# Gated linear attention and a low-rank mixer: the first batch's attention written in another order, halves of units one step behind, the mixer's start in pieces

## The chip, the cores and the metric

The kernel runs on one core of one Trainium2 chip, in fp32. The metric is device time in microseconds (us), the median of several executions. "PE" is TensorE's matrix unit, "DVE" VectorE, "ACT" ScalarE, "POOL" GpSimd, and "SP" SyncE, which here only issues DMA transfers.

## What is computed

There are 4 batches, 8 heads, 768 positions, a head width of 48, a model width of 384 and a mixer rank of 32. The attention keeps a 48x48 state for each head, which a gate of its own for each row lets decay, and reads it with q:

```python
f = 1.0 / (1.0 + np.exp(-f_logit))
for t in range(S):
    state = f[:, :, t, :, None] * state + np.einsum('bhd,bhe->bhde', k[:, :, t], v[:, :, t])
    y[:, :, t] = np.einsum('bhd,bhde->bhe', q[:, :, t], state)
```

The heads side by side are x (4, 768, 384), and the mixer follows:

```python
xt = x.transpose(0, 2, 1)
h = xt @ U @ V                                # U 768x32, V 32x768
u = x + h.transpose(0, 2, 1)
ch = np.maximum(u @ w_ch1, 0.0) @ w_ch2       # 384x1536 and 1536x384
return u + ch
```

## The kernel before

**Units and their pieces.** The work of the attention is cut into 16 units. Unit n is one pair of heads of one batch, four units (`HP`) for each batch. A unit has a front, `prepare(n)`, and a rear, `attend(n)`, and each returns a list of functions, its pieces.

The front has five pieces:

- `gates`: the gate logits f are turned so that time runs along the free axis, and ACT makes the sigmoid `fz` of them. In the first two batches PE does the turning with six transposes (`on_tensor`, L466), and ACT reads PSUM (L487, L488). From batch 2 on (`TURNED`) DVE turns them within SBUF (`turned`, L448), and ACT reads that (L493, L494).
- `keep`: a scan on DVE that runs backwards through each chunk of 64 steps, `X` (L498), with three small DVE operations (L505 to L508) and a small ACT copy (L503).
- `keys`: k turned and multiplied by X, `kz` (L478; from batch 2 on L448 and L481).
- `read_back`: the forward scan `Y` on DVE (L515).
- `queries`: q turned and multiplied by Y, `qT` (L478, or L448 and L481). At its end it issues the transfers of f, k, q and v of unit n+2 on SP (L520, `load` L349), since f, k and q have two buffers.

The rear has five pieces:

- `kept`: PE turns kz back (L568), and ACT copies it to `kb` (L572).
- `states`: ACT spreads the chunks' decays to `whole` (L576), PE forms the chunks' contributions `ds` from kb and v (L584), ACT copies them to `added` (L590), and a DVE scan makes all states `st` (L597).
- `scores`: PE multiplies k and q within each chunk, `sc` (L547), and DVE masks it to `A` (L554).
- `read`: PE reads the states with q, `y` (L612), and ACT makes a small copy, `seen` (L619).
- `inner`: PE adds A times v to the same y (L630), and ACT copies y to `x` (L636).

**The mixer.** The class `Mixer` gives the pieces of a batch. `low_rank` is `ph` on PE (L136) and its copy `h` on ACT (L139). `mix(t)`, for six blocks t of 128 positions, is `pu` on PE (L148), which DVE adds to x (`add`, L144). `turn(t)` is `put`, three transposes on PE (L157), copied to `uT` by ACT (L159). `ch1(a, j)`, for three pairs a of blocks and six j, is `pz` on PE, six matmuls for one (a, j) (L167; the profile has two records of each fp32 matmul), whose positive part ACT writes to `z` (L174). The second product of the first batch is `ch2`, `po` (L189), of which DVE makes the output `o` (L144); later batches use `seven`, `pw` (L212), on sums that DVE forms.

**Weights.** U, V, w1 and w2 come as 8-byte floats. `start` (L51) issues the transfer, and `end` (L56) converts: two ACT operations (L63, L64), three on DVE (L65, L66, L67) and one on POOL (L68), with two buffers `w_y`. `ahead_by` issues the transfer of the ninth weight tile on at each conversion. The first six pieces of w1 land in a buffer of the mixer (`place`, L427), others in four `w_raw`.

**PSUM.** `ps_big` has three buffers for the attention, `ps_mm` two for the mixer.

**What sets the order.** PE's order is the program's order throughout. That of DVE and ACT is the program's in batches 0 and 1 up to the start of the second batch's mixer (the `manual_schedule` at L678); after that a scheduler orders them, and it may also place later work on DVE and ACT among earlier work. SP and POOL are ordered by the scheduler everywhere. `add`, A and st carry a higher priority.

The first batch begins with unit 0's front and unit 1's gates (L681). Then each n takes, in this order (L689):

```python
pieces = [kept, keep, keys, read_back, states, scores, gates, read, queries, inner]
```

where kept, states, scores, read and inner are of unit n, keep, keys, read_back and queries of unit n+1, and gates of unit n+2. For the last n the conversions of U and V stand in the places of the front. Then comes the first batch's mixer, L702: low rank, six `mix`, six `turn`, then `ch1` for all a at each j. Every third of the first thirteen pieces, and each later one, has a weight conversion ahead of it (L703).

In `attention(b, todo)` (L644) the same interleaving, with unit n's rear and unit n+1's front, runs for later batches. Between the pieces `Fill` puts pieces of the previous batch's mixer, in proportion to their cost. `start_mixer` (L662) places the last of those among the `ph`, `pu` and `put` of the batch just attended.

Of the kernel before, what the change touches and what calls it, by code (L numbers as in the profile page):

```python
# [9 lines left out]
F32 = mybir.dt.float32  # L10
# [286 lines left out]
def factored_path(ctx, tc, q, k, v, f_logit, moe_U, moe_V, moe_w_ch1, moe_w_ch2, out, ok):  # L297
# [23 lines left out]
    TURNED = 2  # L321

    assert S % (2 * P) == 0 and H % 2 == 0 and NB < D <= PAD and PAD == 2 * NB and S % NB == 0 and W == NBL * 2 * PAD
    assert DM % P == 0 and FF % P == 0 and FF % WP == 0 and DM == WP and DM <= 512 and R % 32 == 0 and P % R == 0 and P // R <= NBL and NFC % 4 == 0
    assert NBL * PAD <= 512 and C == PAD

    const = ctx.enter_context(tc.tile_pool(name="const", bufs=1))
# [48 lines left out]
                    )  # L376

    load(0, "f", "k", "q")
    load(1, "f", "k")
    load(0, "v")  # L380
    load(1, "q", "v")

    ident = const.tile([P, P], F32, name="ident")
    make_identity(nc, ident)
# [61 lines left out]
    def turned(t, src_tile):  # L446

        nc.vector.transpose(  # L448
            t.rearrange("p (c i) -> p c i", i=NB), src_tile.rearrange("p (c d) -> p c d", d=NB),
        )  # L450
# [3 lines left out]
    def prepare(n):  # L454
# [4 lines left out]
        r, f = raw[n % 2], fz[n % 2]  # L459
        by_chunk = f[:, 0:S].rearrange("p (c t) -> p c t", t=C)  # L460

        def on_tensor(nm):

            pt = ps_big.tile([P, 2, 512], F32, name="pt", tag="big")
            for c in range(NBL):
                nc.tensor.transpose(  # L466
                    pt[:, 2 * c // NBL, c % (NBL // 2) * P : (c % (NBL // 2) + 1) * P],
                    nat[n % 2][nm][:, c].rearrange("p h d -> p (h d)"), ident,
                )
            return pt[:, :, 0 : G * C].rearrange("p a (c t) -> p a c t", t=C)  # L470
# [12 lines left out]
        def gates():  # L483
            f0 = T["f0"] = two.tile([P, NCH], F32, name="f0")
            if b < TURNED:
                pt = on_tensor("f")
                nc.scalar.activation(halves(f)[:, :, :, 1:C], pt[:, :, :, 1:C], AF.Sigmoid)  # L487
                nc.scalar.activation(f0.rearrange("p (a c) -> p a c", a=2), pt[:, :, :, 0], AF.Sigmoid)  # L488
                return
            fT = one.tile([P, S], F32, name="fT")  # L490
            turned(fT, r["f"])
            fv = fT.rearrange("p (c t) -> p c t", t=C)
            nc.scalar.activation(by_chunk[:, :, 1:C], fv[:, :, 1:C], AF.Sigmoid)  # L493
            nc.scalar.activation(f0, fv[:, :, 0], AF.Sigmoid)  # L494
# [14 lines left out]

        def keys():  # L510
            operand("k", "X")

        def read():
            Y = T["Y"] = one.tile([P, S], F32, name="Y")
# [1 line left out]

        def queries():
            operand("q", "Y")
            if n + 2 < NU:
                load(n + 2, "f", "k", "q", "v")  # L520

        return [gates, keep, keys, read, queries]

# [5 lines left out]
    def attend(n):  # L529
# [42 lines left out]
            nc.scalar.copy(kb.rearrange("p h c d -> p h (c d)"), pt[:, :, 0 : NBL * PAD])  # L572

        def states():
            whole = one.tile([P, D, NCH], F32, name="whole")
            nc.scalar.copy(whole, wholes[n % 2].unsqueeze(1).broadcast_to((P, D, NCH)))  # L576

            ds = ps_big.tile([P, 2, 512], F32, name="ds", tag="big")
            for c in range(NBL):
                for s in range(2):  # L580
                    for par in range(2):

                        i = (c + (s & par)) % NBL
                        nc.tensor.matmul(  # L584
                            ds[par * PAD : (par + 1) * PAD, s, c * D : (c + 1) * D],
                            lhsT=T["kb"][part[s ^ par], par, i, :], rhs=vt[part[s ^ par], c, par, :],
                            start=True, stop=True,
                        )

            nc.scalar.copy(  # L590
                added[:, 1:].rearrange("p (e c s) -> p e c s", c=NBL, s=2),
                ds[:, :, 0 : NBL * D].rearrange("p s (c e) -> p e c s", e=D),
            )

            st = two.tile([P, D * NCH], F32, name="st")
            with tc.high_priority(offset=AHEAD):
                nc.vector.tensor_tensor_scan(  # L597
                    st, added[:, 0 : D * NCH], whole.rearrange("p e c -> p (e c)"), 0.0, ALU.add, ALU.mult
                )
            T["st"] = st.rearrange("p (e c) -> p c e", c=NCH)  # L600

# [37 lines left out]
            )  # L639
            del units[n], v_tiles[n]  # L640

        return [kept, states, scores, read, inner]

    def attention(b, todo):  # L644


        fill = Fill(todo, HP * 10)
        for n in range(b * HP, (b + 1) * HP):
            kept, states, scores, read, inner = attend(n)
            if n + 1 < NU:  # L650
                gates, keep, keys, read_back, queries = prepare(n + 1)
                order = [gates, kept, keep, keys, states, scores, read_back, read, queries, inner]
                if (n + 1) // HP >= TURNED:
                    order[0:2] = [kept, gates]
            else:
                order = [kept, states, scores, read, inner]
            for piece in order:
                fill()
                piece()
        fill.rest()  # L660

    def start_mixer(b, after):  # L662
# [14 lines left out]
    ctx.enter_context(tc.manual_schedule(engines={nc.tensor.engine}))  # L677
    with tc.manual_schedule(engines={nc.vector.engine, nc.scalar.engine}):  # L678

        ready = {n: prepare(n) for n in range(2)}  # L680
        for piece in ready[0] + ready[1][:1]:  # L681
            piece()
        for n in range(HP):
            kept, states, scores, read, inner = attend(n)
            _, keep, keys, read_back, queries = ready.pop(n + 1, [lambda: None] * 5)
            if n + 2 < HP:
                ready[n + 2] = prepare(n + 2)
            gates = ready[n + 2][0] if n + 2 < HP else lambda: None
            pieces = [kept, keep, keys, read_back, states, scores, gates, read, queries, inner]  # L689
            if n == HP - 1:  # L690

                pieces[1:4] = loads[: early - 1]
                pieces[-2] = loads[early - 1]
            for piece in pieces:
                piece()
            if n == 0:

                loads = ahead_by(early + FIRST, weights)
        loads = loads[early:]

        m = mixer(0)
        for i, (_, piece) in enumerate(m.before + m.firsts):  # L702
            if loads and (i % 3 == 0 or i >= len(m.before)):  # L703
                loads.pop(0)()
            piece()
        for f in loads:
            f()
        n = len(m.seconds) // (NBL // 2)
        todo, after = m.seconds[:-n], m.seconds[-n:]
        for piece in prepare(HP):  # L710
            piece()
            todo.pop(0)[1]()
        attention(1, todo)
        m = start_mixer(1, after)
        for f in to_sum:
            f()
# [336 lines left out]
```

## Time and profile before

| | us |
|---|---|
| median of 3 runs | 539.18 |
| lowest and highest | 538.66, 539.69 |
| the profiled execution | 539.65 |
| its span | 537.9 |
| PE busy | 504.1 (94%) |
| DVE busy | 268.6 (50%) |
| ACT busy | 144.8 (27%) |
| POOL busy | 33.5 (6%) |
| start of `ph` of the first batch | 56.30 |
| its first `pu`, first `pz`, end of its last `pz` | 59.73, 71.26, 117.96 |
| PE idle before the first `ph`, of 56.3 | 18.1 |
| end of the second batch's last `put` | 208.1 |

The profile is of one execution, and its span leaves out 1.75 us of that execution's time. The page cuts the span into 40 slices of 13.4 us; a digit is the busy share in tenths, and PEclk is the granted clock of TensorE in tenths of full speed. A line of the waits names who waited, for whom, and then the total, how often, and the longest, in us. A line of a timeline has the start, the duration, the engine, the line of the kernel and the operation; in brackets the engine's idle time before it and what ended it. Both engines that matter here show a duration that overlaps with the next by some 0.1 us, so that a series of operations advances by a little less than the sum of its durations.

### The profile page before, as it was taken

What the parts mean: (1) busy time and instruction counts of PE and PEld (TensorE: products, weight loads), DVE (VectorE), ACT (ScalarE), POOL (GpSimd) and SP (SyncE); (2) the same over time, 40 slices, a digit from 0 to 9 for tenths busy, and PEclk for the clock granted to TensorE, in tenths of its full rate; (3) what the DMA queues carried; (4) which work ended last, traced back from release to release, by engine and by line L of the source; (5) the groups of instructions that cost most, each with busy time, mean ns of one, the idle gap of its engine ahead of it and who ended that gap; (6) DMA issues with size and microseconds to landing.
All of it is one profiled execution on the core that took longest, in us unless ns stands there. A gap on an engine that the chain in (4) does not pass through costs nothing.

```text
span 537.9 us, 11981 instructions
## 1 busy us (share of the span) xinstructions
PE 504.1 (94%) x5277; PEld 416.5 (77%) x5277; DVE 268.6 (50%) x406; ACT 144.8 (27%) x293; POOL 33.5 (6%) x49
## 2 busy tenths in 40 slices
PE   5677889999997999999999999999999999999995
PEld 4566378886775547889899777898899868998995
DVE  5675575556667856467575740745403340222232
ACT  3233375561322203232331204220311112202010
POOL 3001243331000000000000000000000000000000
PEclk9875599999999799999999999999999999999999
DMA  9977945524556335032713603010000000000000
GB/s 146 162 155 188 189 114 162 160 78 86 106 88 86 56 63 82 1 56 38 116 22 65 86 0 67 1 24 30 2 2 32 1 30 1 1 29 1 11 20 35
DMA packets 149334, 34.88 MB, mean 65 GB/s; under 512 B 139801, under 2 KB 147481, under 8 KB 149273
## 3 DMA queue, kind: packets, MB, share of 16 engines
q1 hardware_dynamic: 149272, 34.03, 33.6%
q8 instruction: 43, 0.70, 0.6%
q14 instruction: 19, 0.15, 0.1%
HBM read 29.29 MB, written 4.72 MB: 63 GB/s over the span
## 4 chain that ended last, share of the span: by engine, by line
PE 83%; DVE 7%; SPq 4%; ACT 2%; DMA 1%; issue 1%; DVEq 0%; ACTq 0%
PE pz L167 35%; PE pw L212 22%; PE po L189 8%; PE y L612 4%; PE pt L466 3%; PE pu L148 2%; PE y L630 2%; SPq L367 2%; SPq L373 2%; PE ds L584 2%; PE sc L547 1%; PE pt L568 1%; PE put L157 1%; PE ph L136 1%; ACT uT L159 1%
## 5 line engine op out<-in xcount | busy, mean ns | idle before, releaser
L167 PE MATMUL pz<-uT,w 128*128 128x256 f32 x864 | 192.8, 382 | 0.8 <-ACT uT L159 0.7
L167 PEld LDWEIGHTS pz<-uT,w 128*128 128x128 f32 x864 | 162.3, 190 | 23.9 <-ACT uT L159 1.0
L174 ACT ACTIVATE z<-pz 128x512 f32<-128x512 f32 x63 | 37.6, 597 | 130.4 <-PE pz L167 126.3
L212 PE MATMUL pw<-zw,w_raw 128*128 128x192 f32 x324 | 56.2, 328 | 0.8 <-DVE o L144 0.8
L212 PE MATMUL pw<-w,z 128*128 128x192 f32 x324 | 56.2, 328 | 0.0
L212 PEld LDWEIGHTS pw<-zw,w_raw 128*128 128x128 f32 x324 | 52.8, 190 | 2.4 <-DVE o L144 2.1
L212 PEld LDWEIGHTS pw<-w,z 128*128 128x128 f32 x324 | 52.9, 190 | 1.5 <-DVE x L144 0.7
L144 DVE TENSOR_TENSOR w_raw<-z 128x768 f32<-128x768 f32 x18 | 17.2, 953 | 58.7 <-ACT z L174 58.6
L498 DVE TENSOR_TENSOR_SCAN X<-fz,ends 128x768 f32<-128x768 f32 x16 | 28.0, 1750 | 17.7 <-ACT fz L487 13.2
L597 DVE TENSOR_TENSOR_SCAN st<-added,whole 128x576 f32<-128x576 f32 x16 | 21.6, 1351 | 26.4 <-ACT added L590 26.4
L612 PE MATMUL y<-st,qT 48*64 48x48 f32 x704 | 21.2, 275 | 8.4 <-DVE st L597 8.4
L612 PEld LDWEIGHTS y<-st,qT 48*64 48x64 f32 x704 | 18.4, 170 | 12.8 <-issue 11.2
L515 DVE TENSOR_TENSOR_SCAN Y<-fz,starts 128x768 f32<-128x768 f32 x16 | 28.0, 1753 | 0.2
L68 POOL TENSOR_TENSOR w<-w_y,w_r 128x384 int32<-128x384 int32 x24 | 25.3, 1055 | 40.9 <-DVE w_y L67 39.5
L189 PE MATMUL po<-w,zw 128*128 128x384 f32 x72 | 27.2, 524 | 0.0
L189 PE MATMUL po<-w,z 128*128 128x384 f32 x72 | 25.3, 495 | 0.2 <-DVE x L144 0.2
L65 DVE TENSOR_SCALAR w_y<-w_y 128x384 f32<-128x384 f32 (+1 forms) x27 | 11.1, 409 | 27.0 <-ACT w_y L63 27.0
L148 PE MATMUL pu<-h,V 128*128 128x384 f32 x48 | 21.4, 570 | 1.7 <-ACT h L139 0.7
L189 PEld LDWEIGHTS po<-w,zw 128*128 128x128 f32 x72 | 13.8, 201 | 9.0 <-issue 1.8
L144 DVE TENSOR_TENSOR w_y<-w_y,pw 128x192 f32<-128x192 f32 x18 | 6.3, 350 | 28.7 <-PE pw L212 28.7
L144 DVE TENSOR_TENSOR w_y<-x,pw 128x192 f32<-128x192 f32 x9 | 3.2, 350 | 34.3 <-ACT w_y L225 34.3
L148 PEld LDWEIGHTS pu<-h,V 128*128 128x128 f32 x48 | 9.0, 210 | 13.8 <-DVE x L144 7.6
(92 smaller groups left out, 526.2 us busy)
## 6 DMA issues: line engine op xcount, KB each, us to landing
w_raw<-in_moe_w_ch_dram SPq DMA_DIRECT2D x18, 384.0 KB, 3.1
out_dram<-o SPq DMA_DIRECT2D x24, 192.0 KB, 2.1
f_raw<-in_f_logit_dram SPq DMA_DIRECT2D x16, 144.0 KB, 4.0
k_raw<-in_k_dram SPq DMA_DIRECT2D x16, 144.0 KB, 4.2
q_raw<-in_q_dram SPq DMA_DIRECT2D x16, 144.0 KB, 3.9
v_nat<-in_v_dram SPq DMA_DIRECT2D x16, 144.0 KB, 3.3
v_nat<-in_v_dram SPq DMA_DIRECT2D x32, 72.0 KB, 3.1
zw<-in_moe_w_ch_dram SPq DMA_DIRECT2D x6, 384.0 KB, 13.0
```

The lines of the kernel that those rows point to most:

```text
L68: nc.gpsimd.tensor_tensor(dst.bitcast(I32), shaped(y.bitcast(I32)), shaped(r), ALU.add)
L144: nc.vector.tensor_tensor(*args)
L148: nc.tensor.matmul(pm[:, 0:DM], lhsT=V[:, t * P : (t + 1) * P], rhs=h[0], start=True, stop=True)
L167: nc.tensor.matmul(pm[:, i * 2 * P : (i + 1) * 2 * P], lhsT=w1[:, m, o : o + P], rhs=uT[a][:, m, :], start=(m == 0), stop=(m == NDC - 1))
L174: nc.scalar.activation(z[a, c][:, k : k + 2, :].rearrange("p i t -> p (i t)"), pm, AF.Relu)
L189: nc.tensor.matmul(pm, lhsT=z[a, i // NI][:, i % NI, s * P : (s + 1) * P], rhs=w2[:, i, :], start=(i == 0), stop=(i == NFC - 1))
L212: nc.tensor.matmul(pm[:, n * HM : (n + 1) * HM], lhsT=lhs[:, i, :], rhs=rhs[:, i, :], start=(i == 0), stop=(i == NI - 1))
L466: nc.tensor.transpose(pt[:, 2 * c // NBL, c % (NBL // 2) * P : (c % (NBL // 2) + 1) * P], nat[n % 2][nm][:, c].rearrange("p h d -> p (h d) ...
L498: nc.vector.tensor_tensor_scan(backwards(X, S - 1, S), backwards(f, S, S), backwards(ends, S - 1, S), 0.0, ALU.mult, ALU.add,)
L515: nc.vector.tensor_tensor_scan(Y, f[:, 0:S], starts, 0.0, ALU.mult, ALU.add)
L597: nc.vector.tensor_tensor_scan(st, added[:, 0 : D * NCH], whole.rearrange("p e c -> p (e c)"), 0.0, ALU.add, ALU.mult)
L612: nc.tensor.matmul(o(c % 2, par, c // 2), lhsT=T["q"][rows[par], chunk[c]], rhs=T["st"][rows[par], c, :], start=(c <= 2), stop=False, skip ...
```

## The change

No computation is added or left out; the pieces and the transfers come in another order.

1. In the first batch, the scan st becomes a piece of its own (`scan`), and the order becomes: gates of unit 0; then for each n keep(n), scan(n-1), keys(n), scores(n-1), kept(n), read_back(n), queries(n), gates(n+1), read(n-1), inner(n-1), states(n). After the last: scan(3), scores(3), conversion of U, read(3), inner(3), the two conversions of V.
2. The transfer of each of f, k and q of unit n+2 is issued as soon as that tensor of unit n has been turned (`follow`), that of v at the end of a step. At the start, v of unit 0 stands ahead of k of unit 1.
3. The first batch's mixer begins in pieces: low rank, mix 0, 1, turn 0, mix 2, turn 1, mix 3, ch1(0, 0), mix 4, turn 2, mix 5, turn 3, ch1(1, 0), turn 4, turn 5, and then the other `ch1`. A conversion stands ahead of the pieces 1, 5 and each from 7 on, counted from 0.
4. In the later batches, `step(n)` puts the scores, read and inner of unit n-1 beside the kept, states and scan of unit n and the front of unit n+1. The step of unit 4 is on its own, with the first four of the first batch's pieces of `ch2` that are still to do.

```diff
@@ -376,9 +376,9 @@
                     )
 
     load(0, "f", "k", "q")
-    load(1, "f", "k")
+    load(1, "f")
     load(0, "v")
-    load(1, "q", "v")
+    load(1, "k", "q", "v")
 
     ident = const.tile([P, P], F32, name="ident")
     make_identity(nc, ident)
@@ -459,6 +459,11 @@
         r, f = raw[n % 2], fz[n % 2]
         by_chunk = f[:, 0:S].rearrange("p (c t) -> p c t", t=C)
 
+        def follow(nm):
+
+            if n + 2 < NU and n + 2 not in (HP, HP + 1):
+                load(n + 2, nm)
+
         def on_tensor(nm):
 
             pt = ps_big.tile([P, 2, 512], F32, name="pt", tag="big")
@@ -486,9 +491,11 @@
                 pt = on_tensor("f")
                 nc.scalar.activation(halves(f)[:, :, :, 1:C], pt[:, :, :, 1:C], AF.Sigmoid)
                 nc.scalar.activation(f0.rearrange("p (a c) -> p a c", a=2), pt[:, :, :, 0], AF.Sigmoid)
+                follow("f")
                 return
             fT = one.tile([P, S], F32, name="fT")
             turned(fT, r["f"])
+            follow("f")
             fv = fT.rearrange("p (c t) -> p c t", t=C)
             nc.scalar.activation(by_chunk[:, :, 1:C], fv[:, :, 1:C], AF.Sigmoid)
             nc.scalar.activation(f0, fv[:, :, 0], AF.Sigmoid)
@@ -509,6 +516,7 @@
 
         def keys():
             operand("k", "X")
+            follow("k")
 
         def read():
             Y = T["Y"] = one.tile([P, S], F32, name="Y")
@@ -516,8 +524,7 @@
 
         def queries():
             operand("q", "Y")
-            if n + 2 < NU:
-                load(n + 2, "f", "k", "q", "v")
+            follow("q")
 
         return [gates, keep, keys, read, queries]
 
@@ -572,7 +579,7 @@
             nc.scalar.copy(kb.rearrange("p h c d -> p h (c d)"), pt[:, :, 0 : NBL * PAD])
 
         def states():
-            whole = one.tile([P, D, NCH], F32, name="whole")
+            whole = T["whole"] = one.tile([P, D, NCH], F32, name="whole")
             nc.scalar.copy(whole, wholes[n % 2].unsqueeze(1).broadcast_to((P, D, NCH)))
 
             ds = ps_big.tile([P, 2, 512], F32, name="ds", tag="big")
@@ -592,10 +599,12 @@
                 ds[:, :, 0 : NBL * D].rearrange("p s (c e) -> p e c s", e=D),
             )
 
+        def scan():
+
             st = two.tile([P, D * NCH], F32, name="st")
             with tc.high_priority(offset=AHEAD):
                 nc.vector.tensor_tensor_scan(
-                    st, added[:, 0 : D * NCH], whole.rearrange("p e c -> p (e c)"), 0.0, ALU.add, ALU.mult
+                    st, added[:, 0 : D * NCH], T["whole"].rearrange("p e c -> p (e c)"), 0.0, ALU.add, ALU.mult
                 )
             T["st"] = st.rearrange("p (e c) -> p c e", c=NCH)
 
@@ -639,24 +648,44 @@
             )
             del units[n], v_tiles[n]
 
-        return [kept, states, scores, read, inner]
+        return [kept, states, scan, scores, read, inner]
+
+    ahead, here = {}, {}
+
+    def front(n, *names):
+
+        if n >= NU:
+            return []
+        if n not in ahead:
+            ahead[n] = dict(zip(("gates", "keep", "keys", "read_back", "queries"), prepare(n)))
+        return [ahead[n].pop(nm) for nm in names]
+
+    def rear(n, *names):
+
+        if not 0 <= n < NU:
+            return []
+        if n not in here:
+            here[n] = dict(zip(("kept", "states", "scan", "scores", "read", "inner"), attend(n)))
+        return [here[n].pop(nm) for nm in names if nm in here[n]]
+
+    def step(n, fill=lambda: None):
+
+        pieces = rear(n - 1, "scores") + rear(n, "kept") + front(n + 1, "gates", "keep", "keys")
+        made = rear(n, "states", "scan")
+        pieces += rear(n - 1, "read") + [lambda: [f() for f in made]] + front(n + 1, "read_back", "queries")
+        pieces += rear(n - 1, "inner")
+        for piece in pieces:
+            fill()
+            piece()
+        if n + 2 < NU:
+            load(n + 2, "v")
 
     def attention(b, todo):
 
 
         fill = Fill(todo, HP * 10)
-        for n in range(b * HP, (b + 1) * HP):
-            kept, states, scores, read, inner = attend(n)
-            if n + 1 < NU:
-                gates, keep, keys, read_back, queries = prepare(n + 1)
-                order = [gates, kept, keep, keys, states, scores, read_back, read, queries, inner]
-                if (n + 1) // HP >= TURNED:
-                    order[0:2] = [kept, gates]
-            else:
-                order = [kept, states, scores, read, inner]
-            for piece in order:
-                fill()
-                piece()
+        for n in range(b * HP + 1, (b + 1) * HP + 1):
+            step(n, fill)
         fill.rest()
 
     def start_mixer(b, after):
@@ -677,40 +706,47 @@
     ctx.enter_context(tc.manual_schedule(engines={nc.tensor.engine}))
     with tc.manual_schedule(engines={nc.vector.engine, nc.scalar.engine}):
 
-        ready = {n: prepare(n) for n in range(2)}
-        for piece in ready[0] + ready[1][:1]:
+
+        for piece in front(0, "gates"):
             piece()
         for n in range(HP):
-            kept, states, scores, read, inner = attend(n)
-            _, keep, keys, read_back, queries = ready.pop(n + 1, [lambda: None] * 5)
-            if n + 2 < HP:
-                ready[n + 2] = prepare(n + 2)
-            gates = ready[n + 2][0] if n + 2 < HP else lambda: None
-            pieces = [kept, keep, keys, read_back, states, scores, gates, read, queries, inner]
-            if n == HP - 1:
-
-                pieces[1:4] = loads[: early - 1]
-                pieces[-2] = loads[early - 1]
+            pieces = front(n, "keep") + rear(n - 1, "scan") + front(n, "keys") + rear(n - 1, "scores")
+            pieces += rear(n, "kept") + front(n, "read_back", "queries")
+            if n + 1 < HP:
+                pieces += front(n + 1, "gates")
+            pieces += rear(n - 1, "read", "inner") + rear(n, "states")
             for piece in pieces:
                 piece()
-            if n == 0:
+            if n < 2:
+                load(n + 2, "v")
+            if n == 1:
 
                 loads = ahead_by(early + FIRST, weights)
+            elif n > 1:
+                load(n + 2, "f", "k", "q", "v")
+        n = HP - 1
+        for piece in rear(n, "scan", "scores") + loads[:1] + rear(n, "read", "inner") + loads[1:early]:
+            piece()
         loads = loads[early:]
 
         m = mixer(0)
-        for i, (_, piece) in enumerate(m.before + m.firsts):
-            if loads and (i % 3 == 0 or i >= len(m.before)):
+        low, mixes, turns = m.before[:1], m.before[1 : 1 + NBL], m.before[1 + NBL :]
+        start = low + mixes[0:2] + turns[0:1] + mixes[2:3] + turns[1:2] + mixes[3:4] + m.firsts[0:1]
+        start += mixes[4:5] + turns[2:3] + mixes[5:6] + turns[3:4] + m.firsts[1:2] + turns[4:6]
+
+        for i, (_, piece) in enumerate(start + m.firsts[2:]):
+            if loads and (i in (1, 5) or i > 6):
                 loads.pop(0)()
             piece()
         for f in loads:
             f()
         n = len(m.seconds) // (NBL // 2)
         todo, after = m.seconds[:-n], m.seconds[-n:]
-        for piece in prepare(HP):
+        for piece in front(HP, "gates", "keep", "keys", "read_back", "queries"):
             piece()
             todo.pop(0)[1]()
-        attention(1, todo)
+        step(HP, Fill(todo[:4], 7))
+        attention(1, todo[4:])
         m = start_mixer(1, after)
         for f in to_sum:
             f()
```

More of the change, by code (lines that the diff above doesn't have):

```diff
@@ L323, in factored_path @@
     assert S % (2 * P) == 0 and H % 2 == 0 and NB < D <= PAD and PAD == 2 * NB and S % NB == 0 and W == NBL * 2 * PAD
-    assert DM % P == 0 and FF % P == 0 and FF % WP == 0 and DM == WP and DM <= 512 and R % 32 == 0 and P % R == 0 and P // R <= NBL and NFC % 4 == 0
+    assert DM % P == 0 and FF % P == 0 and FF % WP == 0 and DM == WP and DM <= 512 and R % 32 == 0 and P % R == 0 and P // R <= NBL and NFC % 4 == 0 and NBL == 6
     assert NBL * PAD <= 512 and C == PAD
```

## The prediction

> **What bounds the kernel now.** I read the slices of the page first, then the waits of TensorE (PE) and VectorE (DVE) in the stretches that are not full, then the engines' timelines there. All times are microseconds.
>
> ```profile
> PE   5677889999997999999999999999999999999995
> DVE  5675575556667856467575740745403340222232
> PEclk9875599999999799999999999999999999999999
> DMA  9977945524556335032713603010000000000000
> ```
>
> One digit is 13.4. PE is full except in slices 1 to 6, in slice 13 and at the end. So two stretches can give time: the first batch with its mixer's start (0 to 71), and the end of the second batch (168 to 208). After 208 PE idles about 2.2 in all.
>
> Waits of PE from 20 to 72, then of DVE from 7 to 57 (total, times, longest):
>
> ```profile
> PE y L612 <- DVE st L597: 4.9, 3, 2.5
> PE pt L466 <- DMA f_raw<-in_f_logit_dram: 4.3, 1, 4.3
> PE put L157 <- ACT uT L159: 1.3, 2, 0.7
> ```
>
> ```profile
> DVE qT L478 <- PE pt L466: 8.7, 3, 4.1
> DVE X L498 <- ACT fz L487: 5.3, 1, 5.3
> DVE w_y L65 <- ACT w_y L63: 4.9, 3, 2.5
> ```
>
> The first batch ends when DVE has passed its units' scans and products (7.27 to 52.85, 45.6 for about 31 of work): DVE waits 8.7 for q's transpose, because q of unit n+1 is transposed only behind unit n's read, which waits for st, which is DVE's own. `ph` starts at 56.30, the first `pu` at 59.73, the first `pz` at 71.26, the last of the 18 `pz` ends at 117.96. Stretches of that time (PE, PEld, DVE, ACT, POOL busy, clock, DMA share, GB/s):
>
> ```profile
> 41.00:64.80 23.80, 19.02 (x318) 13.10 (x318) 12.14 (x23) 8.96 (x20) 4.69 (x5) 0.50 0.88 177
> 64.80:72.00 7.20, 5.58 (x27) 3.15 (x27) 4.55 (x12) 3.96 (x10) 2.83 (x3) 1.00 0.84 249
> 72.00:118.00 46.00, 46.00 (x215) 40.45 (x214) 25.90 (x56) 26.67 (x55) 18.01 (x18) 1.00 0.40 122
> ```
>
> The clock is half from 41.0 to 64.8, so `ph` and the `pu` are slow: `ph` 2.77 against 1.48 warm, a `pu` 1.15 to 1.28 against 0.65. From 72 on PE is dense: later time comes from when the `pz` start.
>
> At the end of the second batch the read of unit 7 waits 3.5 for a scan that stands behind unit 8's front on DVE:
>
> ```profile
> 168.91 0.84 ACT L493 ACTIVATE fz<-fT 128x756 f32<-128x756 f32 x1
> 169.78 1.76 DVE L498 TENSOR_TENSOR_SCAN X<-fz,ends 128x768 f32<-128x768 f32 x1 [3.28 <-ACT fz L493]
> 172.97 0.96 DVE L481 TENSOR_TENSOR kz<-kz,X 128x768 f32<-128x768 f32 x1
> 173.85 1.35 DVE L597 TENSOR_TENSOR_SCAN st<-added,whole 128x576 f32<-128x576 f32 x1
> ```
>
> PE is then at half clock until 181.6. The stall (3.54), a `po` piece at 4.21 instead of 2.2 and others at half rate (2.6), and five short waits (0.2 to 0.4) at `po`, `pu` and `put` come to about 8.2 until the last `put` ends at 208.1.
>
> [...] fz of unit 8 (168.91) started behind `kb` (168.22), and st behind kz. [...] the units' rows of 192 bytes move at 161 GB/s from 2 to 20, rows of weights at 249 in 64.8 to 72. A tensor of a unit (288 KB) then takes 1.8 to 1.95. [...] 1.75 against 0.95 for a product of the same 128x768, so scans are what DVE is short of.
>
> **The change part by part.** No PE, DVE or ACT operation is added or removed. What moves:
>
> *First batch.* Per unit DVE now does X, the st of the unit before, kz, the A of the unit before, Y, qT. I walked this order with rows of the trace (X 1.75 and three small ones to kz 2.15, kz 0.87, Y 1.67 to 1.75, qT 0.88, st 1.25, A 0.86; PE groups 0.52 to 1.5). X starts at 7.27, then at 14.95, 23.35 and 32.95: the period is 8 to 9.6, of which 7.8 is DVE's own work. qT of unit 0 comes 0.75 later than before (its transpose is behind `kept`); what remains is the transposes of k and q behind `kept` on PE. qT of unit 3 ends at 42.5, st and A of unit 3 at 44.7; read, inner and x follow. `ph` starts at 49.2 with a full clock, 51.4 with half: 5 to 7 earlier. The three conversions of V and U are now around inner 3; h is behind V's on ACT, so the first `pu` starts at t0 = 52.5 to 54.9 against 59.73.
>
> *Loads.* Each f, k, q is issued when its buffer is freed, v after. SP issues the same tensors; at 1.9 each f3 to v3 land by about 33.3, while q of unit 3 is needed at 39.7. I cost this at 0, hidden by 6; if the queue blocked, it would be up to +2.
>
> *Mixer's start.* Before, the `pu`, then `put` ran first with five conversions among them, 11.5 from first `pu` to first `pz`. Now the pieces alternate, and the first `pz` is at t0+6 to t0+9. But from the eighth piece on each has a conversion ahead: w1's third to eleventh. Each is 0.9 on ACT and 1.27 on DVE, so nine are 8.1 and 11.4. In both queues they stand before x4, x5, uT2 to uT5 and the first z. By the walk x4 comes at t0+11.6, x5 at 14.6, uT3 at 15.2, so the second `pz` is at 15.25 and the third at 21.1 (uT5 21.05). Between t0+8.7 and 21.1 PE has some 6 of work (one pz 2.6, two pu 1.3, four put 2.0). The fourth `pz` starts at t0+23.7 (warm) to 27 (half clock in the gaps). Before, the fourth was at 71.26 + 3 x 2.6 = 79.06. So 52.5 + 23.7 = 76.2 or 54.9 + 27 = 81.9: −2.9 to +2.8. I take 0, the middle: the gain of 6 goes into ACT's and DVE's queues. Weights w1 7 to 10 landed at 66.6 to 70.5 before, about when wanted.
>
> *Second batch.* st now has a whole step before its read, so the 3.54 at y is gone. What is late next is DVE. In the changed kernel's built order, unit 10's fT, X, its small operations and Y (5.0 together) stand ahead of the o (sum of x and po) before the six x additions of the second batch's mixer; before, unit 9's front stood there, and DVE still waited 2.46 for PE's `po` before that o (191.44). Counting from unit 4's first transpose, PE reaches the first `pu` at 68.0 (with kept 8 and ds 8, 1.36, already done). DVE has st8 at 63.6, Y9 65.3, fT10 68.75, X10 70.65, Y10 72.75, o at 74.4, first x at 74.9. The second `pu` needs the buffer that o empties: PE waits about 6, then runs at half clock (2.5). The last `put` ends at 92.3 against 90.1: +2.2, less 1.36 done early = +0.8. Bounds: 0 (DVE 2 earlier than walked) and +2.5.
>
> *Batches 2 and 3.* PE is full; each unit's read lies one step later, with more cover. Of the 2.2 of idle some may go: −0.3, between −1 and +0.4.
>
> Sum: 0 + 0.8 − 0.3 = +0.5 on the profiled execution's 539.65 (span 537.9 and 1.75 around it): 540.15. That execution is 0.47 above the median of 539.18, so 539.7.
>
> **Rivals.** About 0.2% (1.1) is what a measurement here can tell from no change: 538.1 to 540.3 is "same".
>
> A, likeliest (0.40): the first batch's gain is given back in the mixer's start, and the y stall becomes a `pu` stall. 539.7; its own range 537.5 to 542.
>
> B (0.32): the first batch is denser[...]: fourth `pz` at 76.2 (−2.9), and DVE is less late in the second batch than walked, where removing the 3.5 and its half clock then leaves −1.0. With −0.3: −4.2, 535.0. For it: DVE waits of 8.7 for q and PE waits of 4.9 for st vanish on their own. Against: even now three waits for w_y behind ACT show the start to be ACT's and DVE's.
>
> C (0.28), slower: one mechanism, the clock. [...] the clock is half and PE's pieces take double, the fourth `pz` comes at t0+27 with t0 54.9 (+2.8), and the same in the second batch's longer stall, +2 instead of +0.8. +2.8 + 2 − 0.3 = +4.5, 543.7. [...] For it: the clock was half from 41 to 64.8 with PE 80% busy by the profile; against: at full clock from 64.8 to 72 PE was only 78% busy.
>
> That the change doesn't do what it says would be that the first batch is bound by its loads (DMA share over 1 until 30). f of unit 2 came late at 19.98, but X of unit 2 stands at 23.35; the walk leaves 6 for q3. I give it no chance of its own.
>
> **How the numbers follow.** A splits 0.10 faster, 0.20 same, 0.10 slower; B is faster, C slower: faster 0.42, same 0.20, slower 0.38. B reaches down to about 533, C up to about 546; leaving out a third of each (0.2 in all) gives 534.4 to 544.4.
>
> **What would show it.** `ph` at 49 to 51.5, not 56.3; no waits of PE for st over 2 in the first batch. First `pz` by 64, but over 4 of PE idle between first and third `pz`, with DVE or ACT as releaser (uT, x). The fourth `pz` at 76 to 82. In the second batch no wait of y for st over 1, and one of about 6 of `pu` for o. PEclk under 9 in slices 5 and 6 and near 185 to 195. I am wrong if the fourth `pz` lies outside 75 to 83, if no `pu` wait over 3 shows in the second batch, or if a wait for the units' loads over 2 appears after 24.

## The result, and the profile after

The changed kernel takes 545.95 us (median of 4 runs, 544.4 to 547.39) against 538.92 before (median of 4). The ratio is 1.0136, with a 95% interval of 1.0091 to 1.0181: slower by 1.4%. The profiled execution took 547.06 us, with a span of 545.2.

The slices of the page after, in the same order as those of before:

```profile
PE   4878759999999789999999999999999999999995
...
DVE  4785775534578974675666551644132340222231
...
PEclk9886778999999989999999999999999999999998
DMA  9977955502467751242533400010000000000000
```

PE is now thinner in slice 6 (68 to 82 us), 5 where it was 8. That is the mixer's start of the first batch, not its attention. The same milestones in both traces give the account in us:

| | before | after | moved by |
|---|---|---|---|
| start of `ph`, first batch | 56.30 | 52.17 | −4.1 |
| first `pu` | 59.73 | 55.61 | −4.1 |
| last `pz` of the first batch ends | 117.96 | 124.56 | +6.6 |
| last `put` of the second batch is over (next `pz` starts) | 208.00 | 217.24 | +9.2 |
| end of the span | 537.9 | 545.2 | +7.3 |

So the first batch gained 4.1, the stretch from `ph` to the last `pz` lost 10.7 (72.4 instead of 61.7), the second batch lost 2.6 and the rest gained 1.9. Unit 8's `kept` and `ds` (1.5) are now done in the second batch and not in the third. Less that, the second batch lost 1.1 and batches 2 and 3 gained 0.4.

PE's waits in the first 75 us after (total, times, longest). The 4.9 for f is the start of the kernel:

```profile
PE pt L575 <- DVE kz L483: 6.0, 3, 2.3
PE pt L471 <- DMA f_raw<-in_f_logit_dram: 4.9, 1, 4.9
PE pz L167 <- ACT uT L159: 3.3, 1, 3.3
PE sc L554 <- issue: 1.6, 1, 1.6
PE pu L148 <- ACT uT L159: 1.6, 1, 1.6
PE y L621 <- DVE st L606: 1.1, 1, 1.1
```

And of DVE's waits:

```profile
DVE st L606 <- ACT added L597: 6.2, 3, 3.9
...
DVE qT L483 <- PE pt L471: 0.8, 1, 0.8
```

The waits for st and for q's transpose are small, as foreseen. But others came in their place: PE's 6.0 for kz and DVE's 6.2 for `added`, neither of which was there before. PE's idle time before `ph` fell by 2.2, from 18.1 to 15.9; about as much of the 4.1 comes from PE being busy for less time (36.3 instead of 38.2), with a higher mean clock (0.85 instead of 0.77).

In the mixer's start, waits of 1.6 and 3.3 (and 1.95 at 81.38) for the turned copies uT are new. ACT's timeline after shows what stands ahead of such a copy (start, duration):

```profile
66.00 0.55 ACT L63 ACTIVATE w_y<-zw 128x384 f32<-128x384 f32 x1
66.44 0.55 ACT L64 ACTIVATE w_r<-zw 128x384 int32<-128x384 uint32 x1
66.89 0.54 ACT L63 ACTIVATE w_y<-zw 128x384 f32<-128x384 f32 x1
67.32 0.54 ACT L64 ACTIVATE w_r<-zw 128x384 int32<-128x384 uint32 x1
67.77 0.46 ACT L159 COPY uT<-put 128x384 f32<-128x384 f32 x1
69.11 0.56 ACT L63 ACTIVATE w_y<-zw 128x384 f32<-128x384 f32 x1 [0.88 <-POOL w L68]
69.56 0.54 ACT L64 ACTIVATE w_r<-zw 128x384 int32<-128x384 uint32 x1
71.44 0.55 ACT L63 ACTIVATE w_y<-w_raw 128x384 f32<-128x384 f32 x1 [1.34 <-POOL w L68]
71.90 0.54 ACT L64 ACTIVATE w_r<-w_raw 128x384 int32<-128x384 uint32 x1
72.34 0.46 ACT L159 COPY uT<-put 128x384 f32<-128x384 f32 x1
```

uT3, the copy at 72.34, could have been made when its `put` ended at 69.5. It stood behind two conversions, and these waited 0.88 and 1.34 for POOL, since both w_y were still in use. POOL and DVE at that time show why it takes so long:

```profile
70.42 0.99 POOL L68 TENSOR_TENSOR w<-w_y,w_r 128x384 int32<-128x384 int32 x1 [1.35 <-DVE w_y L67]
...
69.32 0.36 DVE L66 TENSOR_SCALAR w_y<-w_y 128x384 uint32<-128x384 uint32 x1
...
70.58 1.05 DVE L66 TENSOR_SCALAR w_y<-w_y 128x384 uint32<-128x384 uint32 x1
```

The same operation takes 0.36 alone and 1.05 where it falls beside POOL's addition (70.42 to 71.41); it then ends at 71.63, 0.2 after POOL's. Why the operation takes longer there, the trace does not say. Conversions that follow each other without a gap thus come every 1.95 us by POOL's starts (70.42, 72.37), not every 1.27, and every 2.35 where DVE also makes an addition to x between them (68.07, 70.42).

PE's clock was near half after these waits. Stretches of the trace after (PE, PEld, DVE, ACT, POOL busy, clock, DMA share, GB/s):

```profile
65.00:71.70 6.70, 2.90 (x13) 1.45 (x11) 4.97 (x11) 3.98 (x9) 2.98 (x3) 0.95 0.89 256
71.70:78.50 6.80, 5.65 (x15) 4.36 (x15) 4.68 (x8) 2.37 (x6) 2.98 (x3) 0.54 0.31 85
78.50:81.90 3.40, 1.09 (x5) 0.81 (x5) 2.50 (x5) 2.91 (x8) 0.99 (x1) 0.92 0.55 136
81.90:85.30 3.40, 3.40 (x11) 2.73 (x10) 2.53 (x5) 0.91 (x2) 1.61 (x2) 0.58 0.70 219
```

Here two stretches with PE busy for 2.90 of 6.70 (65 to 71.7) and for 1.09 of 3.40 (78.5 to 81.9) are each followed by one near half clock (0.54; 0.58), although PE is then mostly busy (5.65 of 6.80; 3.40 of 3.40). The second `pz` took 5.34 in a stretch with a mean clock of 0.54; in the kernel with late conversions below it took 2.86 at a clock of 1.00 (65 to 71.7).

### The profile page after: what moved, and what is told of

It is laid out like the page before. It is cut to its first block, busy times and chain, and to the rows that moved or that the text cites. A ratio compares the mean times of both kernels' runs of the same rounds, so it can differ in the third digit from the quotient of the medians.

```text
span 545.2 us, 11991 instructions
## 1 busy us (share of the span) xinstructions
PE 504.9 (93%) x5277; PEld 419.2 (77%) x5277; DVE 273.8 (50%) x406; ACT 145.7 (27%) x293; POOL 31.2 (6%) x49
## 4 chain that ended last, share of the span: by engine, by line
PE 79%; DVE 11%; ACT 4%; DMA 2%; issue 2%; SPq 2%; POOL 0%; DVEq 0%; ACTq 0%; POOLq 0%
PE pz L167 36%; PE pw L212 22%; PE po L189 5%; PE pt L471 3%; PE y L621 3%; PE pu L148 2%; DVE X L505 2%; PE y L639 2%; PE ds L591 2%; PE sc L554 2%; PE pt L575 1%; DVE st L606 1%; DVE Y L523 1%; DMA f_raw<-in_f_logit_dram 1%; SPq L373 1%
## 5 line engine op out<-in xcount | busy, mean ns | idle before, releaser
L167 PE MATMUL pz<-uT,w 128*128 128x256 f32 x864 | 198.8, 389 | 5.8 <-ACT uT L159 5.7
L167 PEld LDWEIGHTS pz<-uT,w 128*128 128x128 f32 x864 | 165.0, 194 | 30.4 <-ACT uT L159 6.3
L212 PE MATMUL pw<-w,z 128*128 128x192 f32 x324 | 56.3, 329 | 0.0
L144 DVE TENSOR_TENSOR w_raw<-z 128x768 f32<-128x768 f32 x18 | 17.2, 955 | 55.2 <-ACT z L174 55.2
L148 PE MATMUL pu<-h,V 128*128 128x384 f32 x48 | 23.0, 596 | 5.4 <-ACT h L139 1.7
L68 POOL TENSOR_TENSOR w<-w_y,w_r 128x384 int32<-128x384 int32 x24 | 24.0, 998 | 39.6 <-DVE w_y L67 39.6
L189 PE MATMUL po<-w,zw 128*128 128x384 f32 x72 | 25.1, 492 | 0.0
L159 ACT COPY uT<-put 128x384 f32<-128x384 f32 x24 | 11.1, 476 | 51.6 <-PE put L157 51.6
L561 DVE TENSOR_TENSOR A<-sc,causal 128x768 f32<-128x768 f32 x16 | 15.2, 949 | 19.1 <-PE sc L554 19.1
L65 DVE TENSOR_SCALAR w_y<-w_y 128x384 f32<-128x384 f32 (+1 forms) x27 | 12.3, 454 | 24.0 <-ACT w_y L63 24.0
L579 ACT COPY kb<-pt 128x768 f32<-128x768 f32 x16 | 12.7, 797 | 35.4 <-PE pt L575 35.4
L621 PEld LDWEIGHTS y<-st,qT 48*64 48x64 f32 x704 | 17.2, 154 | 5.5 <-issue 3.7
```

The source lines that it names most:

```text
L68: nc.gpsimd.tensor_tensor(dst.bitcast(I32), shaped(y.bitcast(I32)), shaped(r), ALU.add)
L144: nc.vector.tensor_tensor(*args)
L148: nc.tensor.matmul(pm[:, 0:DM], lhsT=V[:, t * P : (t + 1) * P], rhs=h[0], start=True, stop=True)
L167: nc.tensor.matmul(pm[:, i * 2 * P : (i + 1) * 2 * P], lhsT=w1[:, m, o : o + P], rhs=uT[a][:, m, :], start=(m == 0), stop=(m == NDC - 1))
L189: nc.tensor.matmul(pm, lhsT=z[a, i // NI][:, i % NI, s * P : (s + 1) * P], rhs=w2[:, i, :], start=(i == 0), stop=(i == NFC - 1))
L212: nc.tensor.matmul(pm[:, n * HM : (n + 1) * HM], lhsT=lhs[:, i, :], rhs=rhs[:, i, :], start=(i == 0), stop=(i == NI - 1))
```

## The experiments

Every kernel was timed against the kernel before on the same chip; the median of before was 538.9, 539.4 and 538.6 us in the three groups. Each group ran on another chip, so a difference between kernels of two groups carries up to 0.8 us of that; the ratios don't. A trace is of one execution. The theories are named in the first expectation. Line numbers of a profile are those of its own kernel.

**Where the loss is: the mixer's start put back.** The changed kernel with the loop of before:

```diff
...
-        for i, (_, piece) in enumerate(start + m.firsts[2:]):
-            if loads and (i in (1, 5) or i > 6):
+        for i, (_, piece) in enumerate(m.before + m.firsts):
+            if loads and (i % 3 == 0 or i >= len(m.before)):
```

> The changed kernel with the start of the first batch's mixer as before (all six pu, all six put, then the pz; five conversions among the first thirteen pieces). The traces put the loss there: the first pu came 4.1 us earlier than before, the last pz 6.6 us later, so 10.7 us were lost between them. Theory 1 (conversions: nine weight conversions stand on ACT and VectorE ahead of the turned copies) and theory 2 (the alternation of pu, put and pz in two PSUM buffers leaves PE waiting) both expect the 10.7 back: about 535 us. Theory 3 (the new first batch hands the mixer a half clock, and any start would be slow after it) expects less than 4 us back: 542 or more.

Measured: 535.8 us, ratio to before 0.9948 (0.9922 to 0.9973). Of the changed kernel's 545.95, 10.15 came back. Here `ph` started at 52.82 and took 2.77, and the last `pz` ended at 115.42, 62.6 later, 0.9 more than in the kernel before (61.7), whose `ph` took 2.77 too, at a clock of 0.50 (56.3 to 59.7). The 0.9 is the first `pu`'s wait for h, 1.60 instead of 0.66. Theory 3 falls.

**The pieces alone.** The reverse edit, on the kernel before.

> The kernel before with only the mixer's start in pieces. Theories 1 and 2: about 10.7 us slower than before, 549 to 550. Theory 3: at most 4 us slower, 543 or less, since the first batch is the old one.

Measured: 549.43 us, ratio 1.0190 (1.0167 to 1.0214), 10.5 slower. PE waited for uT 1.58, 3.33 and 1.96 as in the changed kernel (5.3 in two at `pz`, 1.6 at `pu`). The loss comes with the pieces and is there with the old first batch as well.

**Order of pieces or conversions: the conversions later.** The pieces stay as in the change:

```diff
-            if loads and (i in (1, 5) or i > 6):
+            if loads and (i in (1, 5, 12) or i > 13):
                 loads.pop(0)()
+                if loads and i > 18 and i % 3 == 0:
+                    loads.pop(0)()
```

> The changed kernel, pieces in the same order, but the conversions of w1's third tile and on wait until the turns are done: at the pieces 1, 5, 12 and from 14 on, with two at every third piece from 21 on. Theory 1: uT3 and uT5 come soon after their put, the third pz ends some 20 us after the first pu and not 31, total 535 to 538. Theory 2: PE still waits between the pieces, 543 or more.

Measured: 535.65 us, ratio 0.9953 (0.9935 to 0.9971). Of PE's timeline in this kernel, the second and third `pz`, and unit 4's transpose after the last:

```profile
67.58 2.86 PE L167 MATMUL pz<-uT,w 128*128 128x256 f32 x12 [0.57 <-ACT uT L159]
...
72.75 41.71 PE L167 MATMUL pz<-uT,w 128*128 128x256 f32 x192 [1.08 <-ACT uT L159]
114.30 0.82 PE L471 MATMUL pt<-ident,f_raw 128*128 128x128 f32 x6
```

And the same in the changed kernel:

```profile
72.85 5.34 PE L167 MATMUL pz<-uT,w 128*128 128x256 f32 x12 [3.33 <-ACT uT L159]
...
81.38 43.35 PE L167 MATMUL pz<-uT,w 128*128 128x256 f32 x192 [1.95 <-ACT uT L159]
124.56 0.82 PE L471 MATMUL pt<-ident,f_raw 128*128 128x128 f32 x6
```

The third `pz` ends at about 75.4 (72.75 and 2.65 for a piece at full clock), 20.4 after the first `pu` (55.02), as theory 1 said. From `ph` (51.59) to the last `pz` it is 62.7, 9.7 less than in the changed kernel. Of these 9.7, 5.3 are waits (PE's waits from the first `pu` to the third `pz` are 7.7 in the changed kernel and 2.4 here), 2.5 are the second `pz` at half clock, 1.6 the dense `pz` after it (43.35 against 41.71), and 0.3 small ones. Theory 2 falls: with the same pieces in the same order, most of the waits and the half clock after them are gone (clock 1.00 from 65 to 78.5). The pieces by themselves also bring nothing: 62.7 against 62.6 with the old start, which even has 0.9 more of wait for h in it.

**Why the conversions are so slow: three buffers w_y.** In the changed kernel:

```diff
-            y = pool.tile([P, WP], U32, name="w_y")[0:rows, 0:n]
+            y = pool.tile([P, WP], U32, name="w_y", bufs=3)[0:rows, 0:n]
...
-            h[0] = two.tile([P, DM], F32, name="h", bufs=1)
+            h[0] = three.tile([P, DM], F32, name="h", tag="o")
...
```

> The changed kernel with three buffers w_y instead of two (h shares the buffers of o to make room). In the changed kernel's mixer start ACT waits 3.3 us in four places for GpSimd to empty a w_y. Theory 1a (the depth of the conversions' buffers stretches the queue): these waits go, uT3 and uT5 come earlier, 3 to 8 us faster than the changed kernel (538 to 543). Theory 1b (the mere number of conversions ahead of the copies, on VectorE at 1.3 to 2 us each): VectorE keeps the same rate, so 0 to 2 us faster (544 to 546).

Measured: 540.78 us, ratio 1.0034 (1.0017 to 1.0050), 5.2 faster than the changed kernel. ACT's wait for POOL fell from 3.3 to 1.0 and PE's longest wait for uT from 3.33 to 1.97. POOL's additions still came every 1.95 to 2.35 (68.40, 70.35, 72.70, 74.65). So the conversions were no faster; ACT was held by them less, and its copies got through. Of PE's timeline, the second and third `pz`:

```profile
68.49 4.32 PE L167 MATMUL pz<-uT,w 128*128 128x256 f32 x12 [0.99 <-ACT uT L159]
...
76.02 41.71 PE L167 MATMUL pz<-uT,w 128*128 128x256 f32 x192 [1.97 <-ACT uT L159]
```

The wait of 1.97 is as long as the changed kernel's 1.95, and PE's two transposes ahead of it are the same (0.49 and 0.55 in both). Yet the dense `pz` after it took 41.71, as with late conversions, and not 43.35. What made the difference is not shown.

**The same, without POOL.** The conversion leaves out the lowest bits, and with them ACT's second operation and POOL's addition.

```diff
...
-            nc.scalar.activation(r, lo, AF.Copy, scale=2.0**-29)
...
-            nc.vector.scalar_tensor_tensor(y, hi, 0xC0000000, y, ALU.bitwise_and, ALU.bitwise_or)
-            nc.gpsimd.tensor_tensor(dst.bitcast(I32), shaped(y.bitcast(I32)), shaped(r), ALU.add)
+            nc.vector.scalar_tensor_tensor(dst.bitcast(U32), shaped(hi), 0xC0000000, shaped(y), ALU.bitwise_and, ALU.bitwise_or)
```

> The changed kernel with a shorter conversion: ACT's second operation and GpSimd's addition are left out (the lowest three bits of the weights are then dropped), VectorE writes the weight itself. Each conversion is then 0.45 us on ACT and 1.27 on VectorE, the price that the prediction put on VectorE's part. Theory 1a (GpSimd at the end of the conversion stretches it, by holding buffers and by slowing VectorE beside it): PE's waits for uT shrink by more than half, the third pz ends about 21 to 24 us after the first pu, total 536 to 540. Theory 1b: VectorE's 1.27 for each of nine is enough to keep it late, 542 or more.

Measured: 538.71 us, ratio 0.9991 (0.9977 to 1.0004). In its trace PE's waits for uT are 0.70, 1.76 and 1.08. The first `pu` is at 53.97 and the third `pz` ends at 76.4, 22.4 later. The prediction's walk has this end, which is the start of the fourth `pz`, at 23.7 with a full clock. That is within 1.3 us, though not quite at the walk's price: ACT's part is half of the walk's 0.9. The walk's 1.27 on DVE is what the changed kernel shows where no addition of POOL falls beside a conversion (the first operations of two in a row start at 52.52 and 53.78, 1.26 apart, and at 79.29 and 80.56, 1.27). Theory 1b falls, and 1a stands, with three limits. The edit relieves ACT as well as POOL, so the two are not told apart here. This trace is of the fastest of 12 executions (536.38). And by the ratios the kernel is still 2 us slower than that with late conversions (0.9991 against 0.9953), so part of the loss stays without POOL. The wait of 1.76, for one, follows a wait of ACT of 1.27, until 67.66, for a transfer of w1.

**The first batch: contributions of unit 3 earlier.**

```diff
-            pieces += rear(n - 1, "read", "inner") + rear(n, "states")
+            pieces += rear(n, "states") + rear(n - 1, "read", "inner") if n == HP - 1 else rear(n - 1, "read", "inner") + rear(n, "states")
```

> The changed kernel with the contributions ds of unit 3 ahead of the read and inner of unit 2. In the changed kernel the scan of unit 3 waits 3.9 us for them, with PE at half clock. If VectorE's wait sets the end of the first batch: ph 2.5 us earlier. If PE's own work at half clock does (42 to 51 without a gap over 1.1): ph only 0.6 us earlier, 545 to 546 in all. I expect the second.

Measured: 544.07 us (540.65 to 546.14), ratio 1.0091 (1.0061 to 1.0122). The profiled execution is one of 542.7. In it `ph` started at 52.73, neither 2.5 nor 0.6 earlier than 52.17. DVE's wait only moved: the scan of unit 3 waited 2.1, and then A of unit 3 waited 3.9 for PE's scores. That fits PE as what ends the first batch, but it is not a clean test: in this trace the read and `inner` of unit 3 took some 1.5 each (from 48.50 and 50.34), in the changed kernel's 1.23 and 1.20 (from 48.65 and 50.15), where the clock was 1.00 between 47.2 and 50.6.

The median lies 1.9 under the changed kernel's, but the intervals overlap, and PE's waits for uT were the same (1.57, 3.35, 1.96). The dense `pz`, from 80.15, took 41.71 instead of 43.35. So after the same waits their time differs between executions by 1.6. Whether this makes the spread of the times is not shown: it is 3.0 us for the changed kernel and 5.5 here, but also 4.0 with the mixer's start put back, where PE's longest wait for uT is 0.7.

**The later batches alone.** The kernel before with only part 4 of the change.

> The kernel before with only the later batches' order changed (scores, read and inner of unit n-1 beside the front of n+1 and the first half of n). From the two traces: the second batch's end +1.1 us after taking off work already done, batches 2 and 3 -0.4: 539.6 us, that is +0.7. If the order of the later batches carried more of the loss, it would be +3 or more: 542.

Measured: 539.05 us, ratio 1.0003 (0.9994 to 1.0011). No difference that can be measured. The stall of 3.5 at the read of unit 7 is gone, and waits of 5.0 in all have come up elsewhere (PE from 120 to 240 us): 2.0 at issue, and

```profile
PE pt L568 <- DVE qT L478: 1.8, 2, 1.3
PE pu L148 <- DVE o L144: 1.2, 1, 1.2
```

**The hoisted front: unit 10 behind the mixer's start.** On the kernel with late conversions, the first step of batch 2 is also written out in the program's order:

```diff
...
         for f in to_sum:
             f()
+        fills[2] = Fill(m.main, HP * 10)
+        step(2 * HP + 1, fills[2])
```

> The changed kernel with the late conversions (535.65 us) and with the first step of batch 2 written out as well, so that on VectorE and ACT the front of unit 10 stands behind the second batch's mixer start and not in it. If the hoisted front is what makes pu wait (1.04 for h, 1.18 for o): 2 to 2.5 us faster, 533 to 534. If those waits have another cause or the work is only moved: within 0.5 us of 535.65.

Measured: 532.95 us (532.27 to 533.14), ratio 0.9888 (0.9861 to 0.9915), 2.7 less than the median without the edit (3.5 by the ratios). The two waits of `pu` are gone, and the six `pu` run in one group of 4.84. This is the fastest kernel here, 6 us below the kernel before.

**The first batch alone.** The kernel before with only parts 1 and 2 of the change.

> The kernel before with only the first batch's order and its transfers as in the change; mixer start and later batches as before. From the run with the mixer start put back (535.8) and the later batches alone (+0.15): about 535.6, 3.3 us faster than before. If the gain needs the later batches' order too: 537 or more.

Measured: 535.1 us (533.31 to 536.71), ratio 0.9921 (0.9900 to 0.9942), 3.5 faster.

**The old mixer's start in the fastest kernel.**

> The fastest kernel so far (late conversions, unit 10's front behind the mixer start: 532.95 us), but with the first batch's mixer start as before and not in pieces. From ph to the last pz the two starts took 62.6 us (as before) and 62.7 us (pieces, late conversions), so the pieces are worth nothing: 532.3 to 533.7. If the pieces are worth something of their own once the conversions are out of the way: 534 or more.

Measured: 533.39 us (532.44 to 535.82), ratio 0.9911 (0.9882 to 0.9941). The unit 4 transpose after the last `pz` began at 113.84, with the pieces at 113.65. The medians' ratios differ by 1.2 us, and the intervals overlap: the pieces bring nothing that can be measured.

**The order of the transfers.** In the fastest kernel:

```diff
     load(0, "f", "k", "q")
-    load(1, "f")
+    load(1, "f", "k")
     load(0, "v")
-    load(1, "k", "q", "v")
+    load(1, "q", "v")
...
         def follow(nm):

+            if nm == "q":
+                for one_of in "fkq":
+                    late(one_of)
+
+        def late(nm):
+
             if n + 2 < NU and n + 2 not in (HP, HP + 1):
```

> The fastest kernel so far (532.95 us), but with the units' transfers in the order of the kernel before: k of unit 1 ahead of v of unit 0, and f, k and q of unit n+2 issued together after unit n's q. If the transfers' order costs or brings nothing, as the prediction had it: 532.4 to 533.5. If f of unit 2 is late again as in the kernel before (PE waited 4.3 us for it there): 1 us or more slower.

Measured: 534.06 us (532.09 to 535.38), ratio 0.9921 (0.9904 to 0.9938). The median is 1.1 above the fastest kernel's (1.8 by the ratios), but the intervals of the two overlap. In the trace there was no late f: PE turned f of unit 2 at 20.70 without a wait (20.55 in the fastest kernel), and `ph` began at 51.61 (51.34). A cost of the transfers' order is not shown; up to some 2 us of it stays open.

## Why the prediction was wrong

The forecast was 539.7 with a range to 544.4; it came to 545.95, and the rival that ends slower (543.7, by the clock) was the nearest.

*First batch: right in kind, short by 1 to 3.* The waits for q and st went, as said. `ph` came 4.1 earlier and not 5 to 7, at 52.17, 0.8 past the later end. The walk held up to qT of unit 3, which ended at 43.3 (walked 42.5). Then st and A of unit 3 ended at 49.4 and not 44.7: st waited 3.9 for `added`, whose contributions PE formed from 44.95 on at half clock (0.50 from 43.8 to 47.2). The walk had DVE as the bound there, and no such wait. The run with unit 3's contributions earlier fits PE as the bound, but does not prove it.

*Mixer's start: the step that failed.* The prediction put "Each is 0.9 on ACT and 1.27 on DVE, so nine are 8.1 and 11.4." into the queues, got the third and fourth `pz` at t0+21.1 and t0+23.7 to 27, and took the middle, 0, as the stage's net. It was +6.6. The order of events was right: the conversions stand before uT3 and uT5, and PE waits for ACT between the first and third `pz` (7.2 in four waits, foreseen as over 4; the walk itself has about 6 of idle there). What was wrong is the size of three terms, each beyond the end that the walk allowed:

- *The conversion.* It was priced without POOL and without the release of its two buffers. A conversion took 1.95 and not 1.27 on DVE, since one of DVE's operations took 1.05 beside POOL's addition and not 0.36, and ACT waited 3.3 for buffers ahead of its copies. So the second `pz` came at t0+17.2 and not 15.25: 2.0. With three buffers 5.2 us came back, without POOL (and with less on ACT) 7.2, with the conversions out of the way 10.3.
- *The clock after the waits.* The second and third `pz` ran near half clock (0.54 from 71.7 to 78.5, 0.58 from 81.9 to 85.3), 2.5 and 1.6 more: 4.1 in all. The walk had 0 or 3.3, so its middle holds 1.65. The third `pz` started at t0+25.8, the fourth at about t0+30 (ACT took the third's result at 85.92).
- *The start.* t0 was 55.6, 1.9 past the middle of 52.5 to 54.9.

Against the middle these are 2.0, 2.5 and 1.9, about 6.4 of the 6.6. The run with late conversions shows that the first two hang together: without conversions ahead of the copies, the waits shrink (2.4 instead of 7.7) and the half clock does not come (1.00 from 65 to 78.5).

The price could be read before. In the trace of the kernel before, where its conversions follow each other in the dense `pz`, POOL's additions are 1.95 apart, and DVE's operation between them takes 1.04:

```profile
73.09 0.99 POOL L68 TENSOR_TENSOR w<-w_y,w_r 128x384 int32<-128x384 int32 x1 [1.38 <-DVE w_y L67]
75.04 1.00 POOL L68 TENSOR_TENSOR w<-w_y,w_r 128x384 int32<-128x384 int32 x1 [0.96 <-DVE w_y L67]
...
73.27 1.04 DVE L66 TENSOR_SCALAR w_y<-w_y 128x384 uint32<-128x384 uint32 x1
```

*The clock as a rival.* For this stage rival C describes what the trace shows: a gap of PE (3.33; 1.95), then a piece near half clock (0.54; 0.58). Which gaps bring it was the author's estimate and is not shown: with three w_y the dense `pz` after a gap of 1.97 took no longer than with late conversions (41.71). C's 3.3 (27 instead of 23.7) was short, and t0 came later as well. What it left out is that the conversions make the gaps: with the same pieces and the conversions later, they are mostly gone. Half clock made 4.1 of the 9.7 by which the changed kernel's start exceeds that one's.

*Second batch: the sum right by luck.* +1.1 came, +0.8 was forecast. The y stall was gone, but no wait of 6 for o showed; it was 1.2. DVE was 1.2 later than walked (first x at 76.1 after unit 4's first transpose; 74.9 in the walk). PE was 6.2 later than walked: it reached the first `pu` at 74.2 and not 68.0, and 5.6 of that are small waits for qT, seen, h and at issue, which the walk put at nothing. Writing out the next step took the two `pu` waits away and gave 2.7.

*Batches 2 and 3:* −0.4, forecast −0.3. *Transfers:* costed at 0, and no cost was shown.

*Signs and range.* Two of the prediction's three signs of being wrong appeared: the fourth `pz` came at about 85.9, outside 75 to 83, and no `pu` wait over 3 showed in the second batch. The range stopped at 544.4 since a third of C's reach, up to about 546, was left out, and since the fourth `pz` at t0+27 was held to be the worst. A conversion at 1.95 adds 0.7 for each, some 6 us for nine in DVE's queue; this is an estimate, and not all of it would reach PE.

Two readings in the prediction are slightly off and change nothing: X's first period is 7.7 (7.27 to 14.95), not 8, and near the end of the second batch the clock was full again at 180.9, not 181.6.

## What to carry to other kernels

A chain that crosses engines through few buffers is to be priced by its slowest lap, all engines and the release of the buffer included, before it is put ahead of copies that the busiest engine waits for. Here a queue that was harmless at one lap in 2.6 us of matmuls cost 10 us where the matmuls between were short. If work is cut finer so that an engine starts earlier, look first at what else stands in the queues of the engines that feed it. Where a scheduler may hoist later work into a stage that waits on the same engines, try writing out one step more: here it gave 2.7 us, where the reordering of the later batches gave nothing that could be measured. A forecast that lies in the middle between a good and a bad end needs a reason for the middle.

## What the runs showed of the hardware that was not expected

- In the trace after, a VectorE operation on one 128x384 tensor took 0.36 us alone and 0.98 to 1.20 us where it started during a GpSimd operation of 1.0 us, ending 0.2 after it. Where no GpSimd operation fell beside it, the next conversion followed after 1.26 us (52.52 to 53.78); where one did, after 1.94 (80.56 to 82.50).
- In the same trace, after 3.40 us in which PE was busy for 1.09 (78.5 to 81.9), the next 3.40 ran at a mean clock of 0.58 with PE busy throughout. In the kernel with three w_y, after a wait of about the same length (1.97, and 1.95 here), the dense stretch took 41.71, not 43.35.
- The changed kernel and the one with unit 3's contributions earlier had the same waits there (1.58, 3.33, 1.95 and 1.57, 3.35, 1.96) and differed by 1.6 us in the dense stretch after them (43.35 and 41.71). In the first the clock was 0.58 from 81.9 to 85.3 and 1.00 from there to 124.5.
